# Attention feeding a squared-ReLU FFN: weight-form stores three steps later, two of five differences on GpSimd, Relu and Square one product later

## The chip, the cores and the metric

The kernel runs on one core of one Trainium2 chip. The metric is the device time of one execution in microseconds. The time before is 1417.62 us, the median of three runs (1417.59 to 1418.26). The profile is of another single execution.

The engines are named as the profile names them: PE (TensorE matmul), PEld (TensorE's weight load), DVE (VectorE), ACT (ScalarE), POOL (GpSimd), and SP (SyncE, whose queue issues nearly all DMAs). L12 is line 12 of the kernel before.

## The reference, cut to what matters

```python
# q, k, v: (8, 12, 448, 64), float32; w_in: (768, 2048); w_out: (2048, 768)
q_n, k_n = rmsnorm(q, g_q), rmsnorm(k, g_k)
scores = (1 / sqrt(64)) * q_n @ k_n.T
attn = softmax(scores)
x = (attn @ v) with heads joined            # (3584, 768)
h = maximum(x @ w_in, 0)
out = (h * h) @ w_out                       # (3584, 768)
```

## The kernel before, in words

**Two interleaved streams.** The attention goes through 48 pairs of heads (8 batches, 6 pairs each). The feed-forward part goes through four units of two batches each. While the feed-forward part of unit u runs as a generator (`ffn(u)`), the attention of the next two batches is worked off between its steps: a loop at the end of `program` makes "visits" to a pair (scores, exponentials, attention times values, sums), and calls `run(until)` in between, which advances the generator step by step. The whole program is written under a manual schedule, so each engine works off its instructions in the order in which the Python code emits them.

**What one step of `run` emits.** After each `yield` of the generator, `run` takes one entry of `deep_to_make` (differences of weights), calls `make_sum` (one sum of weights, or a store), then `follow_loads` (loads of weights, and whatever stands in the countdown list `later`), `end_join`, `convert`, and then some entries of the lists `tasks` and `pool_tasks` and some transfers.

**Products in fewer multiplications.** All products of blocks are made by a scheme with seven products P1 to P7 for a two-by-two block matrix, with sums and differences of blocks as operands (`PRODUCTS`, `FIRST_ORDER`). The first unit (u = 0) applies it once; the later units apply it twice for the first matrix (`deep_products`), and need for this ten differences of weights, which the first unit makes and stores to the DRAM tile `in_deep`.

**The first unit.** It has four blocks. Each block takes two tiles of W_in through `first_products` (L970): seven products of three matmuls each into three PSUM banks in rotation. ACT copies P1, P5, P6 and P4 to SBUF (`part`, L979); after P2 and P3 once, after P7 twice, `hidden` emits three instructions: DVE adds or subtracts a bank and a copy into `hid` (L1110), ACT applies Relu in place (L1111), and Square in place (L1112). `hidden_sum` (L1126, POOL) makes the four sums and differences of `hid`, for the first tile during the second tile's products and for the second tile at the start of the second products. The second products (L1140 for the left-over rows, L1202 for the rest) multiply by `out_sb` and are added to `acc` by DVE (L1259).

**Weights, in the first unit only.** Pieces of the weights are loaded as 64-bit words (L1300, L1305), split on ACT (L1319 to L1321) and joined to float32 on DVE (L1332, L1352, L1356). `make_sum` makes four sums per tile (L1432), with DVE and POOL taking turns: for `out_sb` the forms T1, T3, T2 and T4. When they are made, the eight forms of an `out_sb` tile are stored to `out_forms` in one DMA of 1536 KB (L1434), emitted on SP at once; later units load them from there. Per block, `deep_steps` stores five raw forms of W_in to `in_deep` and derives five more in each of two slices of 4 and 3 columns of 128: forms 3, 4, 6, 5 and 9, in this order, each one subtraction or addition (`derive`, L1392, DVE) into a tile `more` of which there are four buffers, each followed one or two steps later by its store (L1410). Forms 5 and 9 depend on no other form.

**The attention's instructions** that the text names: scores L445 (and L434 in later units), exponentials L453 on ACT out of the banks into `wT`, attention times values L535, sums of weights L472 on POOL, the denominators L601 (a matmul with ones into a bank that scores have used), the transposes `kT` and `qT` L366 on DVE, q's gain L368 on ACT, squares L180 on ACT, row sums L193 and L196 on DVE, powers L203 and q's scaling L218 on POOL. L325 issues the transfers of q, k and v, L891 the later units' loads from `in_deep`.

Of the kernel before, what the change touches and what calls it, by code (L numbers as in the profile page):

```python
# [17 lines left out]
AF = mybir.ActivationFunctionType  # L18
# [206 lines left out]
def program(ctx, tc, rows, v, g, wide, ones, moe_w_in, moe_w_out, out, shift):  # L225

    nc = tc.nc
# [76 lines left out]
    def in_blocks(i):  # L304

        return 1 < i < len(pairs) and not alone(i - 2) and not shift
# [359 lines left out]
    def new_parts():  # L666
        return ffn_p.tile([P, 2, S], F32, name="part", tag="part", bufs=2)
# [237 lines left out]
    def turn_roles(*order):  # L905
        roles[:] = [roles[n] for n in order]
# [54 lines left out]
    def first_products(u, p, hid):  # L961

        n = u * NF // 2 + p
        w_sb = in_sb.pop(n)
        copies, rooms = {}, {}
        for name in FIRST_ORDER:
            role, first, left, right = PRODUCTS[name]
            ps = roles[role][:, 0:S]
            for c in range(NK):
                nc.tensor.matmul(  # L970
                    ps, lhsT=w_sb[:, IN.index(left), c, :], rhs=forms[u, c][right],
                    start=first and c == 0, stop=c == NK - 1,
                    skip_group_check=not first,
                )
            if name in ("P1", "P5"):
                rooms[name] = new_parts()
            if name in ("P1", "P5", "P6", "P4"):
                copies[name] = rooms["P1" if name in ("P1", "P6") else "P5"][:, name in ("P6", "P4")]
                nc.scalar.copy(copies[name], ps)  # L979
            if name == "P2":  # L980
                hidden(hid[0][:, 0], ps, copies["P1"], ALU.add)
            elif name == "P3":
                hidden(hid[0][:, 1], ps, copies["P6"], ALU.add)
            elif name == "P7":
                hidden(hid[1][:, 0], ps, copies["P4"], ALU.subtract)
                hidden(hid[1][:, 1], ps, copies["P5"], ALU.add)
            yield COST_IN
        turn_roles(1, 2, 0)

# [118 lines left out]

    def hidden(dst, left, right, op):
        nc.vector.tensor_tensor(out=dst, in0=left, in1=right, op=op)  # L1110
        nc.scalar.activation(dst, dst, AF.Relu)  # L1111
        nc.scalar.activation(dst, dst, AF.Square)  # L1112

    LOWER, UPPER = ds(0, NT * P), ds(S + REST, NT * P)

# [168 lines left out]
    words, targets, sums_to_make, forms_to_store = {}, {}, deque(), deque()  # L1284
# [91 lines left out]
    def deep_steps(blk, upper, lower):  # L1376

        keep = in_deep[blk]

        def raw():  # L1380
            for n, some in enumerate((upper[:, :, 0], upper[:, :, 1], lower[:, :, 1])):
                nc.sync.dma_start(keep[:, :, PLACES[n]], some)
            for n, some in enumerate((upper[:, :, 2], lower[:, :, 2])):
                nc.sync.dma_start(keep[:, :, PLACES[7 + n]], some)

        made = {}

        def derive(some, n, left, right, op):
            size = some.stop - some.start
            made[n] = ffn_p.tile([P, 4, P], F32, name="more", tag="more", bufs=4)[:, 0:size]  # L1390
            left, right = [x() for x in (left, right)]
            nc.vector.tensor_tensor(out=made[n], in0=left, in1=right, op=op)  # L1392
            to_keep.append((keep[:, some, PLACES[n]], made[n]))

        to_keep, steps = deque(), []
        for some in (slice(0, 4), slice(4, 7)):
            a11, a12, a13 = [lambda m=m, s=some: upper[:, s, m] for m in range(3)]
            a21, a22, a23 = [lambda m=m, s=some: lower[:, s, m] for m in range(3)]
            for n, left, right, op in (
                (3, a21, a22, ALU.add), (4, lambda: made[3], a11, ALU.subtract),  # L1400
                (6, a12, lambda: made[4], ALU.subtract), (5, a11, a21, ALU.subtract),
                (9, a13, a23, ALU.subtract),
            ):
                steps.append(
                    lambda s=some, n=n, le=left, ri=right, op=op: derive(s, n, le, ri, op)
                )

        def both(make):
            if len(to_keep) > 1 or not make:
                nc.sync.dma_start(*to_keep.popleft())  # L1410
            if make:
                make()

        return [raw] + [lambda make=make: both(make) for make in steps + [None, None]]
# [11 lines left out]
    def make_sum():  # L1426

        if sums_to_make and callable(sums_to_make[0]):
            sums_to_make.popleft()()
        if sums_to_make:  # L1430
            to, left, right, op = sums_to_make.popleft()
            next(sum_engines).tensor_tensor(out=to, in0=left, in1=right, op=op)  # L1432
        elif forms_to_store:
            nc.sync.dma_start(*forms_to_store.popleft())  # L1434

    pieces, begun = iter(range(len(all_pieces) + 1)), []

# [13 lines left out]
    to_load, later = deque(), deque()  # L1451
# [36 lines left out]
    tasks, pool_tasks, held, gap = deque(), deque(), set(), lambda: None  # L1488
# [45 lines left out]
    def run_all():  # L1534
        before = set(held)
        held.clear()
        while tasks or pool_tasks:
            run_tasks(len(tasks) + len(pool_tasks))
        if not first:
            follow_transfers(len(transfers))  # L1540
        held.update(before)
# [28 lines left out]
    def square(i, x, room, engine=None):  # L1570
        if i <= last:
            ensure("qk", i)
            ensure("qk", i - i % 2)
            rows.square(i, x, room[:, 0 : 4 * P], engine)
# [7 lines left out]
    def weigh_slots(i, n):  # L1582
        if not shift:
            for m in slots_of(i, n):
                score(i, m)
                weigh(i, m)
        elif n:
            weigh_shifted(i)

    def attend_all(i):  # L1590
        slots = range(NJ + 1)
        attend(i, slots)
        add_weights(i, slots)
        forget(i, slots)
        take_sums(i)
        invert(i)
        finish(i)
# [39 lines left out]
    def put_in_order(i):  # L1637
        for x in range(2):
            rescale(i, x)
        if in_blocks(i):  # L1640
            steps = [lambda: store_q(i), lambda: load_blocks(i, 0)]
            for step in steps:
                tasks.extend((lambda: None, lambda: None, step))
# [23 lines left out]
        elif whole(i + 1):  # L1667
            prepare(i + 3)

    def prepare(i):  # L1670

        if i > last:
            return
        room = []
        tasks.append(
            lambda: room.append(io.tile([P, 4 * P], F32, name="squares", tag="squares", bufs=1))
        )
        for x in range(2):
            tasks.append(lambda x=x: square(i, x, room[0]))
            if not first:  # L1680
                tasks.append(gap)
            tasks.append(lambda x=x: rows.add(i, x))
            if not first and i % 2 == 0:
                tasks.append(gap)
        tasks.append(lambda: pool_tasks.append(lambda: put_in_order(i)))
        if in_blocks(i):
            tasks.append(lambda: load_blocks(i, 1))

    def visit_whole(i):
        late = [some for some in tasks if getattr(some, "args", None) == (i,)]  # L1690
        for some in late:
            tasks.remove(some)
        run_all()
        if shift:
            attend_all(i - 1)
            if i <= last:
                weigh_slots(i, 1)
        else:
            if i % 2 == 0:
                both_denominators(i - 2)  # L1700
            for n in range(NJ):
                attend(i - 1, (n,))
                forget(i - 1, (n,))
                if i <= last:
                    score(i, n)
                    weigh(i, n)
                while n == 1 and i % 2 == 0 and late:
                    late.pop(0)()
            if i % 2:
                attend(i - 1, (NJ,))  # L1710
                forget(i - 1, (NJ,))
            join_halves(i - 1)
            if i % 2 == 0:
                tasks.append(lambda: invert_both(i - 2))
                if i <= last:
                    score(i, NJ)
                    weigh(i, NJ)
            if i <= last:
                additions(i)
        tasks.extendleft(reversed(late))  # L1720
        if late:
            tasks.extendleft([gap] * 3)
        if shift or i % 2:
            prepare(i + 3)
        else:
            tasks.append(lambda: tasks.append(lambda: prepare(i + 3)))
        if i <= last:
            tasks.appendleft(lambda: load_v(i))

# [85 lines left out]
```

## Time and profile before

| quantity | value |
|---|---|
| median of 3 runs | 1417.62 us (1417.59 to 1418.26) |
| the profiled execution's own time | 1416.51 us |
| its span | 1414.6 us |
| busy: PE, PEld | 1374.7, 850.2 us |
| busy: DVE, ACT, POOL | 846.8, 586.7, 784.1 us |
| L1392 DVE, `more` from `in_sb`, 128x512 | 12 of 879 ns mean |
| L1392 DVE, `more` from `in_sb`, 128x384 | 12 of 687 ns mean |
| L1110 DVE, L1111 ACT, L1112 ACT | 32 each of 620, 572, 577 ns mean |
| L1434, store of `out_forms` | 8 of 1536 KB, 6.4 us median to landing |
| bytes moved | 229.15 MB, mean 162 GB/s |

The span runs from the first to the last record of the profiled execution; the execution's own time is 1.9 us longer. A group's row gives its number of instructions and the mean duration of one; for an engine's group, the idle time just before its instructions stands beside it with what ended it. A duration counts from an instruction's start, also where it then waits for something that the profile does not show. In a timeline row the columns are start, duration, engine, line, operation, tiles, count, and in brackets the idle time before with its releaser.

### The profile page before, as it was taken

How to read it: one execution, taken by the hardware profiler on the slowest of the kernel's cores; microseconds unless marked ns; L12 is line 12 of the kernel's file. 1: busy time of each engine (PE TensorE's matmuls, PEld its weight loads, DVE VectorE, ACT ScalarE, POOL GpSimd, SP SyncE). 2: the span in 40 equal slices, each digit the busy share in tenths (PEclk: the TensorE clock that was granted, in tenths of full speed). 3: DMA queues.
4: the chain of work that ended last, by engine and by line, in shares of the span. 5: the costliest groups of instructions: out<-in, count | busy, mean ns of one | idle time of the engine just before them, and what ended most of it. 6: DMA issues, size and time to landing. Idle time of an engine off the chain costs nothing.

```text
span 1414.6 us, 19459 instructions
## 1 busy us (share of the span) xinstructions
PE 1374.7 (97%) x6336; PEld 850.2 (60%) x6336; DVE 846.8 (60%) x1675; ACT 586.7 (41%) x1126; POOL 784.1 (55%) x778
## 2 busy tenths in 40 slices
PE   7998999999999999999999999999999999999998
PEld 3333444444444467585766767576676868778694
DVE  4997566887878854355455765445554565344444
ACT  5775466645656234442343434343342403121230
POOL 5667755564655777475575877565573554030311
PEclk9999999999999999999999999999999999999999
DMA  5555845867858866382646747374651726324132
GB/s 143 143 155 161 203 100 147 246 189 182 260 139 260 258 214 176 70 272 67 197 136 195 190 119 248 93 206 126 185 138 42 258 68 234 122 94 175 45 146 81
DMA packets 378931, 229.15 MB, mean 162 GB/s; under 512 B 271940, under 2 KB 347588, under 8 KB 374724
## 3 DMA queue, kind: packets, MB, share of 16 engines
q1 hardware_dynamic: 378528, 227.75, 55.7%
q8 instruction: 52, 0.85, 0.2%
q14 instruction: 59, 0.48, 0.1%
q10 hardware_dynamic: 292, 0.07, 0.0%
HBM read 172.49 MB, written 55.25 MB: 161 GB/s over the span
## 4 chain that ended last, share of the span: by engine, by line
PE 77%; DVE 5%; POOL 5%; DMA 4%; issue 3%; ACT 3%; SPq 3%; POOLq 0%; DVEq 0%; ACTq 0%
PE bank L1202 29%; PE bank L1024 20%; PE bank L1140 5%; PE bank L970 5%; PE bank L434 4%; PE bank L549 4%; PE bank L445 4%; PE bank L535 3%; POOL sum L472 2%; DMA words<-in_moe_w_in_dram 1%; SPq L317 1%; PE bank L610 1%; PE bank L601 1%; ACT wT L453 1%; PE bank L570 1%
## 5 line engine op out<-in xcount | busy, mean ns | idle before, releaser
L1024 PE MATMUL bank<-xT,in_sb 128*128 128x224 f32 x1344 | 289.2, 354 | 4.1 <-ACT part L1013 2.4
L1202 PE MATMUL bank<-out_sb,hid 128*128 128x384 f32 x768 | 269.7, 488 | 3.7 <-DVE acc L1259 3.0
L1259 DVE TENSOR_TENSOR acc<-acc,bank 128x384 f32<-128x384 f32 x324 | 173.2, 548 | 163.7 <-PE bank L1202 137.6
L1024 PEld LDWEIGHTS bank<-xT,in_sb 128*128 128x128 f32 x1344 | 252.6, 190 | 16.1 <-ACT wT L453 5.6
L453 ACT ACTIVATE wT<-bank,rr 128x448 f32<-128x448 f32 x288 | 164.3, 631 | 164.8 <-PE bank L434 100.7
L1202 PEld LDWEIGHTS bank<-out_sb,hid 128*128 128x128 f32 x768 | 144.5, 190 | 108.4 <-DVE acc L1259 6.3
L1202 PE MATMUL bank<-out_sb,sums 128*128 128x384 f32 x576 | 206.0, 490 | 2.0 <-DVE acc L1259 1.9
L203 POOL TENSOR_TENSOR rr<-ms,minus_half 128x8 f32<-128x8 f32 (+1 forms) x96 | 147.8, 1539 | 82.1 <-DVE ms L196 66.9
L1009 DVE TENSOR_TENSOR hid<-hid,bank 128x224 f32<-128x224 f32 x312 | 111.1, 383 | 85.8 <-PE bank L1024 81.9
L1202 PEld LDWEIGHTS bank<-out_sb,sums 128*128 128x128 f32 x576 | 107.7, 190 | 86.6 <-DVE acc L1259 5.6
L970 PE MATMUL bank<-xT,in_sb 128*128 128x448 f32 x336 | 131.9, 546 | 0.3 <-DVE hid L1110 0.3
L472 POOL TENSOR_TENSOR sum<-sum,wT 128x448 f32<-128x448 f32 (+1 forms) x96 | 112.0, 1188 | 9.6 <-ACT wT L453 8.1
L1077 POOL TENSOR_TENSOR hid<-hid 128x448 f32<-128x448 f32 x24 | 27.2, 1142 | 158.2 <-DVE hid L1009 153.8
L445 PE MATMUL bank<-qT,kT 64*128 64x448 f32 (+1 forms) x492 | 106.3, 580 | 5.3 <-ACT part L453 3.1
L472 POOL TENSOR_TENSOR sum<-wT 128x448 f32<-128x448 f32 x48 | 56.7, 1203 | 88.7 <-ACT wT L453 88.7
L970 PEld LDWEIGHTS bank<-xT,in_sb 128*128 128x128 f32 x336 | 62.1, 190 | 69.3 <-issue 59.9
L1140 PE MATMUL bank<-out_sb,hid 128*128 128x384 f32 x256 | 87.6, 488 | 0.0
L1081 ACT ACTIVATE hid<-hid 128x448 f32<-128x448 f32 x96 | 55.0, 573 | 67.6 <-DVE hid L1009 48.5
L434 PE MATMUL bank<-qT,kT 64*64 64x448 f32 x552 | 77.3, 547 | 1.9 <-ACT wT L453 1.9
L1024 PE MATMUL bank<-more,in_sb 128*128 128x224 f32 x288 | 76.2, 357 | 1.5 <-DVE hid L1019 1.5
L445 PEld LDWEIGHTS bank<-qT,kT 64*128 64x128 f32 (+1 forms) x492 | 36.5, 168 | 67.2 <-issue 38.5
L549 PE MATMUL bank<-wT,vt 64*64 64x448 f32 x576 | 75.1, 550 | 0.0
(135 smaller groups left out, 1984.2 us busy)
## 6 DMA issues: line engine op xcount, KB each, us to landing
out_sb<-out_forms SPq DMA_DIRECT2D x24, 1536.0 KB, 10.0
in_sb<-in_deep SPq DMA_DIRECT2D x64, 384.0 KB, 4.2
in_sb<-in_deep SPq DMA_DIRECT2D x80, 256.0 KB, 3.9
words<-in_moe_w_in_dram SPq DMA_DIRECT2D x32, 384.0 KB, 3.7
words<-in_moe_w_out_dram SPq DMA_DIRECT2D x32, 384.0 KB, 3.5
out_forms<-out_sb SPq DMA_DIRECT2D x8, 1536.0 KB, 6.4
qk<-in_q_dram SPq DMA_DIRECT2D x96, 96.0 KB, 2.6
qk<-in_k_dram SPq DMA_DIRECT2D x96, 96.0 KB, 2.7
```

The costliest lines, as they stand in the source:

```text
L203: self.nc.gpsimd.tensor_tensor(out=self.rr[i][:, x, 0 : self.count(i)], in0=ms, in1=self.minus_half.to_broadcast(list(ms.shape)), op=ALU.pow,)
L434: nc.tensor.matmul(sc[ds(half * D, D)], lhsT=turned[i, 1][ds(e * D, D), ds(m * P + half * D, D)], rhs=turned[i, 0][ds(e * D, D), :], start ...
L445: nc.tensor.matmul(sc[some], lhsT=turned[p, 1][r, keys], rhs=turned[p, 0][r, :], start=True, stop=True,)
L453: nc.scalar.activation(new_weights((i, m), e), sc, AF.Exp, scale=rows.rr[i][:, 1, 2 * m + e : 2 * m + e + 1],)
L472: nc.gpsimd.tensor_tensor(out=sums[i, e][some], in0=left[some], in1=weights[key_of(i, m), e][some], op=ALU.add)
L549: nc.tensor.matmul(bank[ds(e * D, D), :], lhsT=values[i][keys, n, e, :], rhs=weights[(i, n), e][keys], start=n == 0, stop=n == NJ - 1 and ...
L970: nc.tensor.matmul(ps, lhsT=w_sb[:, IN.index(left), c, :], rhs=forms[u, c][right], start=first and c == 0, stop=c == NK - 1, skip_group_ch ...
L1009: nc.vector.tensor_tensor(out=quarter(name, n), in0=quarter(base, n), in1=ps, op=ALU.add)
L1024: nc.tensor.matmul(ps, lhsT=left, rhs=right, start=start, stop=stop, skip_group_check=True)
L1140: nc.tensor.matmul(ps, lhsT=hid[a].rearrange("p t e s -> p t (e s)")[:, t, ds(NT * P, P)], rhs=w_sb[t][:, 2 * a + half, :], start=(a, t) = ...
L1202: nc.tensor.matmul(ps, lhsT=lefts[left][:, t, ts(tt, P)], rhs=w_sb[t][:, OUT.index(right), :], start=first and t == 0, stop=t == 1, skip_g ...
L1259: nc.vector.tensor_tensor(out=acc, in0=acc, in1=ps, op=ALU.add)
```

## The change

Three edits, and one that has no effect.

1. In `make_sum`, the store of an `out_sb` tile's forms is no longer issued at once but put into `later` with a count of three. `follow_loads`, which runs right after `make_sum` in the same step, takes one off at each step, and issues the store when the count is zero.
2. In `derive`, forms 5 and 9 are made on GpSimd in place of VectorE: four instructions for each of the four blocks.
3. In `hidden`, the Relu and Square of a result are no longer emitted right after the DVE instruction. They are put on a list, which `end_hidden` empties at the start of the next product of `first_products`, before that product's matmuls; after P7 of a block's second tile it is emptied at once.
4. `prepare` gets an argument `gaps`, which is 0 in every call.

```diff
@@ first_products
         for name in FIRST_ORDER:
+            end_hidden()
             role, first, left, right = PRODUCTS[name]
             ps = roles[role][:, 0:S]
...
                 hidden(hid[1][:, 0], ps, copies["P4"], ALU.subtract)
                 hidden(hid[1][:, 1], ps, copies["P5"], ALU.add)
+            if name == "P7" and p % 2:
+                end_hidden()
             yield COST_IN
@@ hidden
     def hidden(dst, left, right, op):
         nc.vector.tensor_tensor(out=dst, in0=left, in1=right, op=op)
-        nc.scalar.activation(dst, dst, AF.Relu)
-        nc.scalar.activation(dst, dst, AF.Square)
+        to_activate.append(dst)
+
+    def end_hidden():
+        while to_activate:
+            dst = to_activate.popleft()
+            nc.scalar.activation(dst, dst, AF.Relu)
+            nc.scalar.activation(dst, dst, AF.Square)
+
+    to_activate = deque()
@@ derive
-            nc.vector.tensor_tensor(out=made[n], in0=left, in1=right, op=op)
+            engine = nc.gpsimd if n in (5, 9) else nc.vector
+            engine.tensor_tensor(out=made[n], in0=left, in1=right, op=op)
             to_keep.append((keep[:, some, PLACES[n]], made[n]))
@@ make_sum
         elif forms_to_store:
-            nc.sync.dma_start(*forms_to_store.popleft())
+            later.append([3, partial(nc.sync.dma_start, *forms_to_store.popleft())])
@@ prepare
-    def prepare(i):
+    def prepare(i, gaps=0):
...
         room = []
+        tasks.extend([gap] * gaps)
@@ visit_whole
-            tasks.append(lambda: tasks.append(lambda: prepare(i + 3)))
+            tasks.append(lambda: tasks.append(lambda: prepare(i + 3, 0)))
```

## The prediction

> **What bounds the kernel now.** I read the page's busy table first, then TensorE's timeline through the first unit (138 to 505 us, the only stretch that the change touches), then the other engines' timeline around each TensorE stall, then the windows by stage.
>
> ```profile
> PE 1374.7 (97%) x6336; PEld 850.2 (60%) x6336; DVE 846.8 (60%) x1675; ACT 586.7 (41%) x1126; POOL 784.1 (55%) x778
> ```
>
> TensorE bounds the kernel, with 1414.6 - 1374.7 = 39.9 us idle in all. No change off TensorE can give more than the idle time in its own stage. In the first unit the stalls are these (the bracket is the idle time and who ended it):
>
> ```profile
> 268.30 0.97 PE L601 MATMUL bank<-sum,ones 128*64 128x448 f32 x4 [1.31 <-ACT wT L453]
> 287.46 1.92 PE L1202 MATMUL bank<-out_sb,sums 128*128 128x384 f32 x4 [1.54 <-DVE acc L1259]
> 290.61 1.56 PE L1202 MATMUL bank<-out_sb,hid 128*128 128x384 f32 x4 [1.23 <-DVE acc L1259]
> 360.50 0.97 PE L601 MATMUL bank<-sum,ones 128*64 128x448 f32 x4 [0.35 <-ACT wT L453]
> 370.46 0.97 PE L445 MATMUL bank<-qT,kT 64*64 64x448 f32 x4 [0.77 <-ACT qT L368]
> 383.66 1.56 PE L1202 MATMUL bank<-out_sb,hid 128*128 128x384 f32 x4 [1.11 <-DVE acc L1259]
> 454.17 0.97 PE L601 MATMUL bank<-sum,ones 128*64 128x448 f32 x4 [1.31 <-ACT wT L453]
> 473.68 0.91 PE L1202 MATMUL bank<-out_sb,hid 128*128 128x384 f32 x2 [0.70 <-DVE acc L1259]
> 475.28 0.91 PE L1202 MATMUL bank<-out_sb,hid 128*128 128x384 f32 x2 [0.69 <-POOL out_sb L1432]
> ```
>
> With 0.30 at 166.75 and 0.33 at 380.99 they add up to 9.6 us: 3.0 behind ACT, 5.0 behind DVE, 0.8 behind qT, 0.7 behind POOL. That is the ceiling. I number the unit's blocks 0 to 3; first products begin at 139, 231, 325 and 417 us.
>
> The ACT stall of block 1, from the full timeline:
>
> ```profile
> 260.51 1.77 PE L445 MATMUL bank<-qT,kT 64*128 64x448 f32 x8
> 264.23 0.61 DVE L1110 TENSOR_TENSOR hid<-bank,part 128x448 f32<-128x448 f32 x1
> 264.88 0.58 ACT L1111 ACTIVATE hid<-hid 128x448 f32<-128x448 f32 x1 [2.72 <-DVE hid L1110]
> 265.97 2.19 ACT L453 ACTIVATE wT<-bank,rr 128x448 f32<-128x448 f32 x4
> ```
>
> The scores are ready at 262.3, but the four exponentials stand on ACT behind a Relu that waits for a late DVE, and L601 needs the bank they read. And why DVE is late:
>
> ```profile
> 255.27 1.29 POOL L1126 TENSOR_TENSOR sums<-hid 128x384 f32<-128x384 f32 x1 [5.94 <-ACT hid L1112]
> 255.61 1.37 DVE L1432 TENSOR_TENSOR out_sb<-out_sb 128x384 f32<-128x384 f32 x1
> 256.51 2.54 POOL L472 TENSOR_TENSOR sum<-sum,wT 64x448 f32<-64x448 f32 x2
> 256.90 2.37 DVE L1332 TENSOR_SCALAR out_sb<-words 128x384 uint32<-128x384 uint32 x1
> 265.36 0.55 DVE L1432 TENSOR_TENSOR out_sb<-out_sb 128x384 f32<-128x384 f32 x1
> 278.08 0.56 DVE L1392 TENSOR_TENSOR more<-in_sb 128x384 f32<-128x384 f32 x1 [0.75 <-DMA in_deep<-more]
> ```
>
> The same L1432 takes 1.37 us beside a POOL operation and 0.55 us beside none; L1392 also holds DVE while a store frees its buffer.
>
> **What the Trainium skill says.** "SBUF — State Buffer", section "SBUF: two separate sides": DVE operations with two SBUF inputs or in a two-port mode and GpSimd operations take a shared port pair as an exclusive lock for the whole instruction. The trace agrees (1.37 against 0.55). "GPSIMD Engine Reference", section 4.1: a two-input elementwise operation is about twice as slow on GpSimd. It agrees: 1.05 to 1.21 us on POOL (rows L1126 and L1432) against 0.55 us for 128x384. "DMA: Bandwidth & Descriptors", section "Queues, rings and completion order": SP has one row, a ring on each of the 16 DMA engines. So a store of 1536 KB, 6.4 us to landing here, stands ahead of every later load.
>
> **The change, part by part.**
>
> *Relu and Square with the next product.* The same 64 activations (572 and 577 ns). The order of the built program puts the P2 pair of a block's second W_in tile behind the four exponentials (the stall above), and the P3 pair of the first tile behind qT and the exponentials. In blocks 1 to 3 the exponentials then start at the scores' end (262.3 for 265.97). L601's other inputs are long there (the last `sum` ends at 259.05), so the next thing late is nothing: -1.31 - 0.35 - 1.31 = -2.97 us. What waits for the late pair is POOL's hidden_sum and the second products; P7 of the last product is still activated at once, and P7 of the other follows its DVE operations with no visit between, so POOL's start is unmoved. Cost 0; if that cover failed, a pair is 1.15 us late. I keep 0 to +1.2.
>
> *Two of five differences on GpSimd.* DVE loses 8 x 0.879 + 8 x 0.687 = 12.5 us (rows L1392 `more<-in_sb`, which hold 3 as well as 5 and 9) and the waits ahead of them, up to 9.5 us. POOL gains eight 128x384 at about 1.1 us and eight 128x512, not in the trace; scaled from 1.19 for 128x448 I take 1.3 (bounds 1.2 to 1.5): 19.2 us, 4.8 a block. Each also locks the ports against DVE's L1352, L1356, L1332 and L1432, up to about 0.6 us each, so DVE's net relief is from 12.5 + 9.5 down to 12.5 - 16 x 0.6 = 3. On the path, by block:
> - Block 0: DVE sat 6.59 us at 163.38 for a buffer. Now POOL sits there, with `sum` and `rr` behind it, which have until 177. The 0.30 at 166.75 goes.
> - Block 1: the second pair (0.55, 0.75 wait, 0.56 = 1.86 us) leaves between 275.2 and 278.6. But DVE then waits for TensorE at the first L1259 (282.47; L1140 ended at 281.8), so only about 0.65 of relief reaches the 1.54 and 1.23. I take -0.65 (0 to -2.77).
> - Block 2: qT comes earlier, but ACT's Relu ends at 369.39: -0.35 of 0.77. DVE already waited at L1259 (0.31 at 376.18), so the 0.33 and 1.11 stay (0 to -1.44).
> - Block 3: -0.3 of 0.70 and 0.69 (0 to -1.39), since the second is POOL's.
>
> POOL's second pair stands just before the four hidden sums. It needs 2.2 us; the idle time ahead of those sums is 2.92, 2.45 and 3.30. It fits, so I add 0; each microsecond it overruns delays the last out_sb form by as much.
>
> *Stores later.* Eight stores; the first of block 1 moves on SP past seven issues (k, v twice, `in_deep` twice, words, `lasts`), from 269.97 to about 277.8. The words load at 273.93 and the `in_deep` store that frees POOL's buffer lose 1536 KB ahead of them; two k loads, three `in_deep` stores and the words load at 281.11 get it nearer ahead. DMA share between 268 and 284 is 0.92 to 0.97, so those found a backlog anyway. In block 3 the k load behind `kT` L366 is late already (3.21 at 476.83), at a share near 1. An earlier TensorE meets loads that don't come earlier. I charge +1.0 (bounds -1 to +4).
>
> Sum: -2.97 - 0.30 - 0.65 - 0.35 - 0.3 + 1.0 = -3.6 us. Later units are unchanged in order and bound by TensorE, so they keep it. The profiled execution took 1416.51 (span 1414.6): 1412.9. The median shown is 1417.62, 1.1 above that execution, so 1414.0.
>
> **The rivals.**
>
> *All stalls close.* If DVE's relief carries through the second products, -9.3: 1408.3. For it: the chain of waits runs through DVE from 254.75 to 264.85 and, but for 4.75 us of a words load, from 269 to 286. Against: DVE's own wait for TensorE in between. Chance 0.15.
>
> *Given back to transfers.* Words and k loads land at the same absolute time; DVE, in order, waits there longer (words for L1332 at 285.2, k at 476.8). The gains of blocks 1 and 3 (1.96 and 1.61) shrink to a third, with 1.0 from blocks 0 and 2: -2.2, 1415.4. For it: the DMA shares. Chance 0.20.
>
> *POOL becomes the bound, slower.* The last out_sb form (L1432 on POOL) comes later by d, if the pair's buffer or the port lock holds POOL past its gap. TensorE's slack there is 0.9 in block 1 (289.68 to 290.61), about 2.1 in block 2 and none in block 3. Cost (d - 0.9) + (d - 2.1) + d against 3.6: the gain is gone at d = 2.2, and it is slower by over 0.2% (2.8 us) from d = 3.1. At d = 4: 9.0 - 3.6 = +5.4, 1423. For it: the 0.69 stall and POOL busy 4.00 of 4 us in 256 to 264. Against: the gaps, and the store that frees the buffer now stands ahead of 1536 KB. Chance 0.13.
>
> That the change doesn't move what it says is excluded by the built order; TensorE's own order is the same.
>
> **How the numbers follow.** Forecast 0.52, its own range 1411.5 to 1416; rivals 0.15, 0.20, 0.13. About 0.2%, 2.8 us, is what can be told from no change. Of the forecast 0.43 lies below 1414.8 and 0.09 within; so faster 0.43 + 0.15 = 0.58, same 0.09 + 0.20 = 0.29, slower 0.13. The range takes in most of the first rival and all of the second: 1409.5 to 1419.5.
>
> **What would show it.** Right: no idle before L601 behind wT in blocks 1 to 3; `more` on POOL at 1.1 to 1.3 us, ending before the hidden sums; POOL, not DVE, waiting for `in_deep`. L1259 stalls remain in part. Wrong: a growing idle of L1202 behind POOL out_sb L1432 (slower rival), longer DVE waits for words or k (second), or no L1259 stalls (first).

## The result and the profile after

The changed kernel took 1414.18 us (median of 7 runs, 1410.33 to 1418.34), and the kernel before 1417.69 us beside it (7 runs, 1416.47 to 1420.53). The ratio is 0.9972 with an interval of 0.9956 to 0.9988: faster by 0.28%. The profiled execution took 1414.61 us, and its span is 1412.7 us. The predicted 1414.0 us was met within 0.2 us, but not by its own sum: each of its three edits came out otherwise, and a place that it had excluded brought the gain.

The page's busy table of the kernel after:

```profile
PE 1373.6 (97%) x6336; PEld 849.9 (60%) x6336; DVE 847.8 (60%) x1659; ACT 587.9 (42%) x1126; POOL 802.0 (57%) x794
```

POOL has the 16 instructions more and DVE the 16 fewer. Yet DVE's busy time has not fallen (846.8 us before). TensorE's stalls in the first unit of the kernel after, from its timeline (the bracket is the idle time and who ended it; L1212, L1269 and L1443 are L1202, L1259 and L1432 of before):

```profile
281.66 1.93 PE L1212 MATMUL bank<-out_sb,sums 128*128 128x384 f32 x4 [1.42 <-DVE acc L1269]
285.76 2.93 PE L1212 MATMUL bank<-out_sb,hid 128*128 128x384 f32 x4 [2.17 <-DVE acc L1269]
367.81 0.97 PE L445 MATMUL bank<-qT,kT 64*64 64x448 f32 x4 [2.04 <-ACT qT L368]
...
469.61 0.91 PE L1212 MATMUL bank<-out_sb,hid 128*128 128x384 f32 x2 [1.43 <-DVE acc L1269]
472.30 1.02 PE L1212 MATMUL bank<-out_sb,hid 128*128 128x384 f32 x2 [1.78 <-POOL out_sb L1443]
```

The three stalls before the denominators (L601) are gone, as predicted, and so is the 0.30 in block 0. But with 0.31 at 277.39 and 0.92 at 380.22, both behind `acc`, the sum over the unit is 10.1 us where it was 9.6 us. The stalls behind `acc`, `qT` and POOL's `out_sb` have grown by more than the others gave. So the unit cannot be where the time came from. The stages, from the starts of each block's first products (L970) and of the next unit's scores (L434) in the timelines, one profiled execution each; the last three columns are experiments that are told below:

| stage, us | before | after | stores alone | forms on POOL alone | activations alone | stores and activations |
|---|---|---|---|---|---|---|
| start to block 0 | 138.77 | 134.56 | 133.96 | 140.03 | 139.40 | 134.35 |
| block 0 | 91.98 | 91.41 | 91.86 | 91.41 | 91.73 | 92.12 |
| block 1 | 94.61 | 95.90 | 94.48 | 96.93 | 94.74 | 94.02 |
| block 2 | 91.24 | 91.30 | 91.20 | 92.41 | 90.66 | 90.59 |
| block 3 | 89.62 | 91.43 | 89.32 | 89.76 | 89.02 | 90.62 |
| later units | 908.38 | 908.10 | 907.78 | 907.46 | 907.65 | 907.70 |

Between before and after, the stretch before the first unit lost 4.2 us, the first unit took 2.6 us more, and the rest is the same within 0.3 us. Differences of 1 to 3 us between single stages must be read with care: TensorE ran at half its clock for some microseconds of some stages (last section). In the first unit that cost 1.7 us each in blocks 1 and 3 after, in block 1 of the forms alone and in block 3 of stores and activations; ahead of it, 1.7 us before and with the activations alone, and 3.4 us with the forms alone.

**Before the first unit.** Here the attention runs alone, and the first W_out tile is already loaded, joined and summed beside it (the code that works here, `begin`, calls `make_sum` and `follow_loads` just as `run` does); so the first of the eight stores is emitted here. What SP's queue waited for in the kernel before, from 84 to 114 us (total, times, longest, in us):

```profile
SPq L1434 <- POOL out_sb L1432: 6.3, 1, 6.3
```

SP stood for 6.3 us at the store, because POOL had not made the last form, T4. The timeline of before shows what came of it:

```profile
97.72 1.31 POOL L1432 TENSOR_TENSOR out_sb<-out_sb 128x384 f32<-128x384 f32 x1
99.05 0.33 SPq L1434 DMA_DIRECT2D out_forms<-out_sb  x1
99.48 2.02 SPq L317 DMA_DIRECT2D vt<-in_v_dram  x2
...
111.80 0.55 ACT L1319 ACTIVATE words<-words 128x384 f32<-128x384 f32 x1 [7.95 <-DMA words<-in_moe_w_out_dram]
...
113.92 4.07 PE L445 MATMUL bank<-qT,kT 64*128 64x448 f32 x12 [3.14 <-ACT part L453]
```

It reads as a chain. POOL works on a pair's powers (1.88 us) and q (1.11 us) before T4; SP waits for T4; the loads of v, q, k and, at 108.41, of the next words are issued behind it. ACT, in order, sits 7.95 us at the split of these words, with the exponentials behind it, and TensorE waits 3.14 us for a bank that they read. The same stretch after:

```profile
94.56 1.22 SPq L317 DMA_DIRECT2D vt<-in_v_dram  x2
...
102.31 0.38 SPq L1473 DMA_DIRECT2D out_forms<-out_sb  x1
...
105.52 0.57 ACT L1329 ACTIVATE words<-words 128x384 f32<-128x384 f32 x1 [2.11 <-DVE out_sb L1342]
```

The loads go out 4.9 us earlier and the words 6.7 us earlier (at 101.69), and the store goes out behind them (L1473 is the line of `follow_loads`). From 90 to 116 us ACT waits no longer than 0.35 us for a DMA, and TensorE's longest stall from 90 us to the first unit is 0.40 us.

### The profile page after: what moved, and what is told of

Its sections match the earlier page's. It is cut to its first block, busy times and chain, and to the rows that moved or that the text cites. A ratio compares the mean times of both kernels' runs of the same rounds, so it can differ in the third digit from the quotient of the medians.

```text
span 1412.7 us, 19458 instructions
## 1 busy us (share of the span) xinstructions
PE 1373.6 (97%) x6336; PEld 849.9 (60%) x6336; DVE 847.8 (60%) x1659; ACT 587.9 (42%) x1126; POOL 802.0 (57%) x794
## 4 chain that ended last, share of the span: by engine, by line
PE 78%; POOL 5%; issue 4%; DMA 4%; DVE 3%; SPq 2%; ACT 2%; POOLq 0%; DVEq 0%; ACTq 0%
PE bank L1212 30%; PE bank L1027 20%; PE bank L971 7%; PE bank L1150 5%; PE bank L549 4%; PE bank L434 4%; PE bank L445 4%; PE bank L535 3%; POOL sum L472 2%; DMA words<-in_moe_w_in_dram 1%; DMA qk<-in_k_dram 1%; DMA words<-in_moe_w_out_dram 1%; POOL rr L203 1%; PE bank L610 1%; PE bank L570 1%
## 5 line engine op out<-in xcount | busy, mean ns | idle before, releaser
L1212 PE MATMUL bank<-out_sb,hid 128*128 128x384 f32 x768 | 271.3, 490 | 6.6 <-DVE acc L1269 4.8
L1269 DVE TENSOR_TENSOR acc<-acc,bank 128x384 f32<-128x384 f32 x324 | 173.3, 549 | 170.6 <-PE bank L1212 141.2
L1212 PEld LDWEIGHTS bank<-out_sb,hid 128*128 128x128 f32 x768 | 144.9, 191 | 111.9 <-DVE acc L1269 8.6
L1212 PE MATMUL bank<-out_sb,sums 128*128 128x384 f32 x576 | 205.6, 489 | 1.5 <-DVE acc L1269 1.4
L1212 PEld LDWEIGHTS bank<-out_sb,sums 128*128 128x128 f32 x576 | 107.9, 190 | 85.4 <-issue 4.8
L434 PE MATMUL bank<-qT,kT 64*64 64x448 f32 x552 | 75.7, 541 | 1.9 <-ACT wT L453 1.9
L180 ACT ACTIVATE squares<-qk 128x512 f32<-128x512 f32 (+1 forms) x68 | 39.4, 579 | 88.6 <-POOL xT L689 51.1
```

The lines of the kernel that those rows point to most:

```text
L434: nc.tensor.matmul(sc[ds(half * D, D)], lhsT=turned[i, 1][ds(e * D, D), ds(m * P + half * D, D)], rhs=turned[i, 0][ds(e * D, D), :], start ...
L1212: nc.tensor.matmul(ps, lhsT=lefts[left][:, t, ts(tt, P)], rhs=w_sb[t][:, OUT.index(right), :], start=first and t == 0, stop=t == 1, skip_g ...
L1269: nc.vector.tensor_tensor(out=acc, in0=acc, in1=ps, op=ALU.add)
```

## The experiments

All times are medians, each with its ratio to the kernel before and the ratio's interval. Lines of code that aren't shown are as before.

| kernel | us | ratio | interval |
|---|---|---|---|
| stores later, alone | 1410.10 | 0.9949 | 0.9936 to 0.9962 |
| forms 5 and 9 on GpSimd, alone | 1420.09 | 1.0022 | 1.0012 to 1.0031 |
| Relu and Square later, alone | 1415.19 | 0.9994 | 0.9986 to 1.0002 |
| stores and activations | 1410.36 | 0.9956 | 0.9941 to 0.9972 |
| only the first store later | 1409.69 | 0.9954 | 0.9940 to 0.9969 |
| only the other seven later | 1415.77 | 1.0006 | 0.9992 to 1.0020 |
| first store: T4 at once, seven forms later | 1414.06 | 0.9988 | 0.9978 to 0.9997 |
| first store: seven forms at once, T4 later | 1409.84 | 0.9956 | 0.9940 to 0.9972 |
| stores and activations, GpSimd in the first slice | 1412.86 | 0.9976 | 0.9968 to 0.9983 |
| stores and activations, GpSimd in the second slice | 1409.50 | 0.9957 | 0.9941 to 0.9973 |
| all stores at once, first tile's T4 on VectorE | 1410.33 | 0.9963 | 0.9954 to 0.9973 |

### Each edit alone, and two together

*Stores alone* (edit 1):

```diff
-            nc.sync.dma_start(*forms_to_store.popleft())
+            later.append([3, partial(nc.sync.dma_start, *forms_to_store.popleft())])
```

> The kernel before with the later stores alone. Theory A (the gain is SP's: before, SP stands 6.3 us at the first store for a sum on POOL and holds the loads behind it): nearly the whole gain is here, the 3.14 us stall of TensorE at 114 us and the half-clock stretch after it are gone, so -3.5 to -5 us, faster than the changed kernel or equal. Theory B (my forecast's: the gain is the moved activations, stores cost about 1): between -0.5 and +1.5 us. Rival C (the scatter of the runs made it): no stall gone, within 1 us.

It gives 0.51%, more than the whole change. In the table of stages, 4.8 of the profile's 6.0 us lie before block 0. (The count of three is taken down once in the step that emits the store, so the store goes out two steps later.)

*Forms 5 and 9 on GpSimd alone* (edit 2):

```diff
-            nc.vector.tensor_tensor(out=made[n], in0=left, in1=right, op=op)
+            engine = nc.gpsimd if n in (5, 9) else nc.vector
+            engine.tensor_tensor(out=made[n], in0=left, in1=right, op=op)
```

> The kernel before with forms 5 and 9 on GpSimd alone. Theory A: a loss or nothing, 0 to +4 us, with longer stalls of TensorE behind DVE's acc additions and behind POOL's out_sb forms, as in the changed kernel (1.42 and 2.17 in block 1, 1.43 and 1.78 in block 3). Theory B: -1 to -2 us, part of DVE's stalls closed.

It costs 0.22%. In this profile TensorE's stalls in the first unit sum to 11.9 us, where they were 9.6, and the longer ones lie in blocks 1, 2 and 3. In the table of stages the loss shows in blocks 1 and 2, with 1.7 us of block 1 from the slower clock; that block 0 starts 1.3 us later than in the kernel before is not the edit's doing, as none of its instructions runs ahead of that; the slower clock took 1.7 us more there than before. SP's wait of 6.3 us is still there.

*Activations alone* (edit 3, the diff of `first_products` and `hidden` above):

> The kernel before with Relu and Square one product later alone. Theories A and B agree on the three stalls before the denominators (1.31, 0.35, 1.31): they go. B lets TensorE keep all of it: -3.0 us. A expects part of it to come back as longer waits at the second products, which stand behind DVE: -1 to -2.5 us. The stall at 114 us stays in both.

Nothing that these runs can tell from no change, but the 3.0 us of theory B are outside the interval. Its stalls before L601 are gone all the same, and the stalls of the unit sum to 8.7 us for 9.6.

*Stores and activations* (edits 1 and 3):

> The changed kernel with forms 5 and 9 back on VectorE. Theory A: faster than the changed kernel by 1 to 4 us, so -5 to -7 us against the kernel before. Theory B: slower than the changed kernel by 1 to 2 us, about -2 us against the kernel before.

As fast as the stores alone: the intervals cover each other's medians. The three edits taken singly sum to -0.51 + 0.22 - 0.06 = -0.35%, within the interval of the change's -0.28%.

### Which store, and is it the wait or the bytes

*Only the first store later*, and *only the other seven*, with the two branches exchanged:

```diff
-            nc.sync.dma_start(*forms_to_store.popleft())
+            to, dst = forms_to_store.popleft()
+            if dst is out_sb.get(0):
+                later.append([3, partial(nc.sync.dma_start, to, dst)])
+            else:
+                nc.sync.dma_start(to, dst)
```

> The kernel before with only the first of the eight stores three steps later. Theory A: that store makes the whole gain of all eight, -5 to -7 us, and the 3.14 us stall at 114 us is gone. Rival (the gain is spread over the stores, or lies with DMA traffic in blocks 1 to 3): less than half of it, under -3 us.

> The kernel before with the other seven stores three steps later and the first at its old place. Theory A: nothing, within 1.5 us of the kernel before, and SP's 6.3 us wait and the stall at 114 us are still there. Rival (spread over the stores): more than half of the gain of all eight, -3.5 us or more.

One of eight stores holds the whole gain, and the other seven do nothing that can be measured.

*The store's bytes against its wait.* The first store of 1536 KB is cut in two: in one kernel T4's 192 KB, which SP must wait for, stay at the old place, and in the other the seven forms that are made earlier (1344 KB) stay.

```diff
+            if dst is out_sb.get(0):
+                nc.sync.dma_start(to[:, 7:8], dst[:, 7:8])
+                later.append([3, partial(nc.sync.dma_start, to[:, 0:7], dst[:, 0:7])])
+            else:
+                nc.sync.dma_start(to, dst)
```

> The kernel before, with form T4 of the first out_sb tile stored at the old place (192 KB) and its other seven forms three steps later. SP still waits at the old place for POOL's T4, but an eighth of the bytes stands ahead of the loads. Theory A, the wait of SP: the stall at about 114 us stays, and the time is that of the kernel before, within 1 us. Rival A2, the 1536 KB ahead of the loads: the stall goes, -4 us or more.

> The mirror: seven forms of the first tile at the old place (1344 KB) and T4 three steps later. The bytes stay ahead of the loads, and SP waits only for T2 and T3, which are made before 95 us. Theory A, the wait of SP: most of the gain, -3.5 us or more, no stall over 1 us at 114 us. Rival A2, the bytes: as the kernel before, within 1.5 us.

In the kernel with T4 at once SP still waits 6.3 us for POOL. TensorE's stall in its timeline:

```profile
112.06 2.97 PE L445 MATMUL bank<-qT,kT 64*128 64x448 f32 x12 [1.91 <-ACT part L453]
```

With seven eighths of the bytes at the old place and SP's wait there cut to 2.4 us (for VectorE's T2), the gain is whole (0.9956), and the stall is gone. With the wait of 6.3 us kept and seven eighths of the bytes moved, the gain is 0.12%, and the stall falls from 3.14 to 1.91 us. So the bytes without the long wait cost nothing that can be measured, and the wait with an eighth of the bytes makes most of the loss. The bytes add to it only behind the wait, probably because the loads find an emptier queue there; that reason was not tested. The pure theory of the wait (no gain in the first kernel) was too strict.

*A second way to the same end.* All stores stay where they were. Only the last form of the first tile is made on VectorE, so that it doesn't stand behind POOL's powers:

```diff
-            next(sum_engines).tensor_tensor(out=to, in0=left, in1=right, op=op)
+            engine = next(sum_engines)
+            if 0 in out_sb and len(sums_to_make) == 0 and not t4_made:
+                t4_made.append(True)
+                engine = nc.vector
+            engine.tensor_tensor(out=to, in0=left, in1=right, op=op)
```

> The kernel before, all stores at their old places, with one sum moved: T4 of the first out_sb tile from POOL to DVE, where it follows T2. Theory A (SP waits for that sum, which stood on POOL behind a power and a scaling): SP's wait at the first store falls from 6.3 us to about 3, the 1536 KB stay ahead of the loads, and the gain is that of the single later store, -4 us or more, as in the kernel that stores seven forms early. Rival (bytes, or the place of the store on SP): within 1.5 us of the kernel before.

What SP waited for there, and in its timeline what followed the store of 94.77:

```profile
SPq L1439 <- DVE out_sb L1437: 3.0, 1, 3.0
```

```profile
95.20 2.01 SPq L317 DMA_DIRECT2D vt<-in_v_dram  x2
```

The store with all its bytes still stands ahead of the loads; only the wait is 3.3 us shorter, and the loads go out at 95.20 instead of 99.48. The gain is 0.37%, and block 0 starts at 134.51, with the changed kernel (134.56). A wait of 3.0 us on SP costs nothing here that these runs can tell, and one of 6.3 us does: that is the cause by a route that shares no line with the change. The edit also takes one form off POOL, but the gain was whole without that in the kernel that stores T4 later.

### Which of the forms on GpSimd

*Only in the first slice* of four columns (`size == 4`, 128x512), and *only in the second* (`size == 3`, 128x384), each with the stores and the activations of the change:

```diff
-            engine = nc.gpsimd if n in (5, 9) else nc.vector
+            engine = nc.gpsimd if n in (5, 9) and size == 4 else nc.vector
```

> The changed kernel with forms 5 and 9 on GpSimd in the first slice (four columns) only, and on VectorE in the second. It stands between the changed kernel (0.9972) and the one with none on GpSimd (0.9956). Theory P1 (the port lock alone, every GpSimd form costs about the same): half of the way, about 0.9964. Theory P2 (only the second pair harms, since it stands beside DVE's joins ahead of qT and just ahead of the hidden sums): as with none, 0.9956, and the qT stall in block 2 at 0.6 us.

> The mirror: forms 5 and 9 on GpSimd in the second slice only. P1: about 0.9964 as well. P2: as the changed kernel, 0.9972, with the qT stall in block 2 at 2 us and the first slice's DVE joins no longer stretched to 2.3 us.

Both expectations on where the loss lies missed by the medians. It isn't shared evenly, and the second slice isn't the harmful one: with the second alone the time is that of the version without GpSimd forms (0.9957 and 0.9956), and with the first alone 0.9976. The intervals of the two slices overlap from 0.9968 to 0.9973, so the times alone don't settle it. The profiles point the same way. In microseconds, TensorE's stalls in the first unit and the busy time of DVE (the page's), one execution each, all with the stores and the activations of the change:

| forms on GpSimd | TensorE's stalls | DVE busy |
|---|---|---|
| none | 8.0 | 848.7 |
| first slice only | 10.5 | 850.9 |
| second slice only | 7.4 | 843.2 |
| both (the changed kernel) | 10.1 | 847.8 |

With the first slice on GpSimd, DVE has eight instructions fewer and is busy longer; with the second it is relieved, and the stalls don't grow.

## Why the number was right and its reasons were not

**The stretch.** The prediction's first sentence calls the first unit "the only stretch that the change touches". That step failed, and it decided the sign of a term. The store's line runs eight times, and the trace of before has two of these issues ahead of the unit, at 99.05 and 127.93 us. I followed the unit's six and took the charge from the bytes that move in it. The rule that no change off TensorE gives more than the idle time of its own stage failed there too: from 90 us to block 0 TensorE's stalls sum to 3.5 us before and to 1.0 us with the stores alone, and block 0 starts 4.8 us earlier, since the slower clock behind the stall went as well (last section).

**Stores later: forecast +1.0 us (bounds -1 to +4), measured -0.51% (-0.64 to -0.38), 6.6 us by the medians.** For the stores that I looked at, the charge of +1.0 us can't be told from the measurement: the other seven alone measure +0.06% (-0.08 to +0.20), nor can that be told from nothing. The first one's wait was outside the bounds because I looked at DMA traffic behind the store, and not at what the store itself waited for. The wait view of SP's queue before the unit shows it in one line. The bytes ahead of the loads, which the prediction put into its charge, cost nothing measurable where 1344 of the 1536 KB stayed there.

**Relu and Square later: forecast -2.97 us, measured -0.06% (-0.14 to +0.02).** The order moved as told, and the stalls before L601 went. What failed is "the next thing late is nothing". In the kernel with the activations alone, block 1's first products take 44.40 us for 45.77 us, -1.37 us for the -1.31 that was forecast; then its second products take 50.34 us for 48.84 us. The timelines of that kernel show where it went, DVE first and then TensorE:

```profile
278.33 1.19 DVE L1402 TENSOR_TENSOR more<-in_sb 128x384 f32<-128x384 f32 x1 [1.06 <-DMA in_deep<-more]
```

```profile
283.95 1.56 PE L1212 MATMUL bank<-out_sb,hid 128*128 128x384 f32 x4 [1.70 <-DVE acc L1269]
```

TensorE comes earlier to the second products, but DVE does not come earlier to `acc`: its difference waits for a buffer that a store frees (until 278.08 in the kernel before, 278.33 here) and then takes 1.19 us where it took 0.56, and what stands behind it comes no earlier, the first `acc` at 283.35 (282.47 before; the block starts 0.38 us later here). A stall of 1.70 us stands at 283.95 where there was none. This is the rival "given back to transfers", with a store's buffer in the place of a load. Blocks 2 and 3 kept 0.6 us each in this one execution. The three stalls of 2.97 us went, others grew, and the unit's sum fell by 1.0 us, about what the runs show.

**Two of five differences on GpSimd: forecast -0.30 - 0.65 - 0.35 - 0.3 = -1.6 us, measured +0.22% (+0.12 to +0.31), about 3 us.** What was right: the waits for `in_deep` left DVE (9.5 us before, 2.0 us after), and POOL stood 5.7 us for the buffer in DVE's place without harm; block 0 became 0.57 us shorter. What failed is the step from DVE's relief to TensorE. POOL's forms were somewhat longer than forecast: the 128x512 form took 1512 ns where I took 1.3 us (my upper bound was 1.5), the 128x384 form 1116 ns where I took 1.1. These are the groups by shape of the kernel after:

```profile
L1403 POOL TENSOR_TENSOR more<-in_sb 128x512 f32<-128x512 f32 x8 | 12.1, 1512 | 5.7 <-DMA in_deep<-more 5.7
L1403 POOL TENSOR_TENSOR more<-in_sb 128x384 f32<-128x384 f32 x8 | 8.8, 1116 | 0.0
```

DVE's busy time fell by only 0.7 us with the forms alone (846.8 to 846.1), though its instructions on `more` took 10.6 us less; the difference, an estimated 0.6 us for each of the 16 forms, went into its other instructions, which took longer. So the 0.6 us that I took as the most that a form can hold DVE was the average. It fell unevenly, and most of it in the first slice (table above). "SBUF — State Buffer", section "SBUF: two separate sides", says that the loser of the port lock blocks fully. The trace agrees, and where POOL has no gap between its instructions a single DVE instruction pays more than a microsecond. POOL and then DVE around block 1's first slice, in the timelines of the kernel after:

```profile
255.34 1.59 POOL L1403 TENSOR_TENSOR more<-in_sb 128x512 f32<-128x512 f32 x1
256.88 1.00 POOL L1443 TENSOR_TENSOR out_sb<-out_sb 128x384 f32<-128x384 f32 x1
257.83 1.32 POOL L1136 TENSOR_TENSOR sums<-hid,sums 128x384 f32<-128x384 f32 x1
259.12 1.39 POOL L1403 TENSOR_TENSOR more<-in_sb 128x512 f32<-128x512 f32 x1
260.46 1.31 POOL L1136 TENSOR_TENSOR hid<-hid 128x384 f32<-128x384 f32 x1
261.74 0.99 POOL L1443 TENSOR_TENSOR out_sb<-out_sb 128x384 f32<-128x384 f32 x1
```

```profile
255.93 2.37 DVE L1366 CUSTOM_DVE_ANT_0 out_sb<-words,out_sb 128x768 uint16<-128x768 uint16 x1
...
260.84 2.31 DVE L1362 SCALAR_TENSOR_TENSOR out_sb<-words,out_sb 128x384 uint32<-128x384 uint32 x1
```

The same two instructions with the forms on DVE (stores and activations only):

```profile
257.83 1.14 DVE L1366 CUSTOM_DVE_ANT_0 out_sb<-words,out_sb 128x768 uint16<-128x768 uint16 x1
...
261.56 0.55 DVE L1362 SCALAR_TENSOR_TENSOR out_sb<-words,out_sb 128x384 uint32<-128x384 uint32 x1
```

In the ten microseconds from 253 to 263 DVE is busy in both, with 8 instructions in the kernel after and 11 in the other, though two of the 11 are the forms that the edit takes away. So it does less useful work there, not more, and what follows is late: the first form of the second slice starts 37.80 us after the block in the kernel after, and 36.84 us in the other. Block 2 shows one consequence to the hundredth: measured from the block's start, DVE transposes `qT` at 366.43 - 321.87 = 44.56 us in the kernel after and at 363.60 - 320.49 = 43.11 us in the other, 1.45 us later, and TensorE's stall behind `qT` is 2.04 for 0.59 us, 1.45 more. In block 3 the rival "POOL becomes the bound" is seen in part: 1.78 us before the last `out_sb` form of POOL, 0.69 before, and 1.77 in the kernel with the second slice alone, so there my "it fits, so I add 0" failed. That rival's own price, 5.4 us slower, wasn't reached: blocks 1 and 2 show no stall behind POOL. Of the 3 us of the forms alone, 2.3 us are longer stalls in its one profile, and by the estimate below about 0.6 us is slower clock.

**The sum.** -7.2 us (the interval's centre, -0.51% of 1416.7) - 0.8 + 3.1 = -4.9 us singly, -3.5 us measured together, -3.6 us forecast. The forecast came near because its terms were missed in opposite directions: the stores by -8, the activations by +2 and the forms by almost +5 us. That is luck, not a right sum. (The prediction's split of the 9.6 us of stalls has a slip too: those behind DVE are 5.2 us, not 5.0.)

## What to carry to other kernels

Before costing a DMA that is moved, list every one of its issues over the whole program, and read what each waits for on its queue: a store that waits for its data holds every load issued behind it, and here one such wait of 6.3 us cost more than all the bytes. Where two engines share a port lock, work moved from the faster to the slower one can cost the faster as much time as it saves, as 10.6 us less brought 0.7 us here; count instructions done per microsecond on the engine that is to be relieved, not its busy time. A stall that goes is only worth what the next late engine leaves, so follow the relieved engine to its next partner and ask what fixes that partner's time.

## What the runs showed of the hardware

After some stalls TensorE runs at half its clock for some microseconds. The windows of the kernel before, behind the stall of 3.14 us (window, length, busy time of PE, granted clock, DMA share, GB/s):

```profile
112.00:114.00 2.00, 0.08 (x1) 1.00 1.05 241
114.00:116.00 2.00, 2.00 (x4) 0.61 0.68 152
116.00:118.00 2.00, 2.00 (x11) 0.54 0.48 159
```

And of the kernel after, behind the stalls of 1.42 and 2.17 us in block 1:

```profile
284.00:286.00 2.00, 0.24 (x1) 0.81 0.49 155
286.00:288.00 2.00, 2.00 (x4) 0.50 0.63 172
288.00:290.00 2.00, 2.00 (x10) 0.84 1.07 246
```

In the first, 2 x 0.39 + 2 x 0.46 = 1.7 us of work are lost on top of the stall; in the second, 2 x (0.19 + 0.50 + 0.16) = 1.7 us, less what falls in idle time. So the stall at 113 us costs 3.14 + 1.7 = 4.8 us, which covers the 4.2 us by which block 0 starts earlier. It happened behind (or from the end of) the stall of 3.1 to 3.2 us in each of the four profiles that have it (before, forms alone, activations alone, the other seven stores), and in two of these four (forms alone, the other seven stores) the stretch was twice as long, with 3.4 us lost. It happened behind shorter ones sometimes: behind 1.45 and 0.68 us at 468 and 469 with stores and activations, and behind 1.5 us in block 1 with only the first store later, for twice the length (granted clock 0.81, 0.50, 0.50, 0.50 and 0.98 in the windows of 2 us from 282 to 292). That covers the 2.3 us by which block 1 took longer in that kernel (96.88) than before (94.61), with the same instructions. But it was not behind the 2.04 us at 368 after, not behind the 1.91 us at 112 with T4 at once, and not behind the 1.91 us at 509 after, though it was behind the 1.89 us at 510 before. "TensorE: Matmul & The Clock Gate", section "Part 1: The HAM clock gate (the "warmup" mystery)", names a half clock after at least one idle window of about 3.4 us, and a free-running window. The length of the slow stretch agrees (1.7 us lost at half speed is 3.4 us, and 3.4 us lost is twice that); the idle time needed doesn't, since 3.14 us and less were enough here.

How much of the gain is clock? Every run on record has its mean granted clock. The share that was not granted, times the span, estimates the time lost in that run (to about 1.4 us, since the clock is given to 0.001). The means over the runs:

| kernel | runs | lost to the clock, us (estimate) |
|---|---|---|
| before, beside the stores alone | 35 | 6.5 |
| stores alone | 5 | 1.7 |
| only the first store later | 6 | 2.1 |
| seven forms at once, T4 later | 6 | 1.9 |
| first tile's T4 on VectorE | 22 | 2.8 |
| T4 at once, seven forms later | 22 | 4.8 |
| only the other seven later | 14 | 6.6 |
| forms 5 and 9 on GpSimd alone | 14 | 7.1 |

So of the 6.9 us by which the means of the kernel before and of the stores alone differ, about 4.8 us are clock that is no longer lost, and the stall itself is the smaller part. That is more clock than the one stretch of 1.7 us in the profile of before. Two of the four profiles with the stall have twice that behind it; where the rest was lost, a profile of one execution can't say.

Single runs of one kernel scatter by several microseconds (after: 1410.33 to 1418.34), and the scatter goes with the clock: of the 35 runs of the kernel before, the eight with a clock of 0.994 or less have a median of 1418.1 us, and the ten with 0.997 or more one of 1414.9 us. No experiment changed the clock by itself.
